# All transfers of a grouped-attention backward kernel on GpSimd's queue, small scalings on VectorE

## The chip, the cores and the metric

The kernel runs on one core of one Trainium2 chip. The metric is the device time of one execution in microseconds. The kernel before was run six times: 726.22 to 735.26, median 733.89. One further execution was profiled; every line of a profile below is from it.

A core has five instruction streams: TensorE (PE: matrix products and transposes; its weight loads are shown as PEld), VectorE (DVE), ScalarE (ACT), GpSimd (POOL) and SyncE (SP). Each runs its own instructions in order and waits on semaphores for the others. Transfers between main memory (HBM) and the on-chip memory SBUF are issued by an engine into a queue and carried out by 16 DMA engines that all queues share. In this kernel SP's transfers go out on a queue that the profile lists as "hardware_dynamic" (q1) and GpSimd's on one that it lists as "software_dynamic" (q0).

## The reference

Attention with 32 query heads that share 4 key/value heads, and its gradients:

```
B, Hq, Hkv, Sq, Sk, D = 32, 32, 4, 4, 2048, 128
scores = einsum("bhqd,bhkd->bhqk", q, repeat(k)) * D ** -0.5
p      = softmax(scores)
out    = einsum("bhqk,bhkd->bhqd", p, repeat(v))
out, vjp = jax.vjp(forward, q, k, v);  dq, dk, dv = vjp(grad_out)
```

It returns out, dq, dk and dv, all bf16. k, v, dk and dv are 32 x 4 x 2048 x 128, 67 MB each: 136 MB are read and 136 MB written. q, grad_out, out and dq are small.

## The kernel before

**The work.** One batch is one pass. Its 32 x 4 query rows fill the 128 partitions, 32 rows for each key/value head. A batch loads q and grad_out (`LQ`, two transfers of 32 KB, lines 430 and 432), four k tiles and four v tiles (`LK`, `LV`, 512 KB each, line 438: 128 rows of 4096 bytes). TensorE transposes k and v (`KT`, `VT`, line 452), multiplies scores (`S`, line 463), VectorE takes the maximum (`MX`, line 470), ScalarE the exponential (`EX`, line 479), VectorE the sum of each row and its reciprocal rinv (`L`, lines 483 and 485). Then come out (`O`, line 514), delta, the row sum of out times grad_out (`DL`, line 529), dp (`DP`, line 463), ds (`DS`, line 536), and dq, dv and dk.

The division by the softmax's sum is folded into small operands. `dop` is grad_out times rinv (line 488), `qp` is q times rinv times the scale (line 491), `rs` is rinv times the scale (line 495), a single column. `dop` is an operand of every dv product, `qp` of every dk product (`DV`, `DK`, line 551), and `rs` scales dq when it leaves PSUM (`DQe`, lines 521 and 523). All three are computed on GpSimd.

The products land in PSUM (eight banks). VectorE and ScalarE share the copies from there to SBUF: `KTe`, `VTe`, `ETe`, `DTe` (lines 420 and 423) and the casts of dv and dk (`DVe`, `DKe`, line 556: 128 x 1024, f32 to bf16). A batch's dv and dk leave in two stores of 1 MB each (`DVs`, `DKs`, line 560: 128 partitions, two rows of 4096 bytes each), its out and dq in one of 32 KB each (`Os`, `DQs`, line 525).

**The order.** `plan` runs once, when the program is built: it simulates the units of all 32 batches against due times (`DUE`), buffer counts (`CAP`) and costs (`OCC`), and returns one list of units. `emit` writes each unit's instructions in the order of that list, so the list sets the order on every engine. Work of neighbouring batches overlaps: the dk products of one batch run beside the scores of the next.

Transfers of one queue stand in the order of the list. SP has q, grad_out, k, v, dv and dk, 14 a batch; in the steady state one batch's worth is q, go, one v, two dv, four k, three v, two dk. GpSimd has per batch qp, dop, rs, the store of out and the store of dq. Of the transfers of one queue each waits, besides what its own buffers need, for the completion of the eighth transfer before it. SP waits in order: while it stands at a store whose casts are not done, the loads behind it are not issued.

Of the kernel before, what the change touches and what calls it, by code (L numbers as in the profile page):

```python
# [13 lines left out]
ALU = mybir.AluOpType  # L14
# [350 lines left out]
def kernel(  # L365
# [11 lines left out]
    nc = tc.nc  # L377
# [7 lines left out]
    scale = float(D) ** -0.5  # L385
# [18 lines left out]
    q_r, go_r, o_r, dq_r = rows(q), rows(grad_out), rows(out_0), rows(out_1)  # L404
    k_r, v_r, dk_r, dv_r = keys(k), keys(v), pairs(out_2), pairs(out_3)
    flat = lambda t: t[:].rearrange("p c d -> p (c d)")
# [18 lines left out]
    def emit(u):  # L425
        b, name, arg = u.key[0], u.key[1], u.key[2:]
        t = T[b]
        if name == "LQ":
            t["q"] = sm_pool.tile([P, D], BF16, name="q_sb")
            nc.sync.dma_start(out=t["q"][:], in_=q_r[b])  # L430
            t["go"] = sm_pool.tile([P, D], BF16, name="go_sb")
            nc.sync.dma_start(out=t["go"][:], in_=go_r[b])
        elif name in ("LK", "LV"):
            h, = arg
            p_, src = (k_pool, k_r) if name == "LK" else (v_pool, v_r)
            x = p_.tile([P, C, D], BF16, name="k_sb" if name == "LK" else "v_sb")
            t[name[1], h] = x
            nc.sync.dma_start(out=flat(x), in_=src[b, h])
        elif name == "QT":
            ps = t["qtp"] = bank(b, "qt", dt=BF16)  # L440
            nc.tensor.transpose(out=ps[:, 0, :], in_=t["q"][:], identity=ident[:])
# [11 lines left out]
        elif name in ("KTe", "VTe"):  # L453
            copy16(u.on, t[(name[:2],) + arg][:], t[(name[:2] + "p",) + arg][:])
        elif name in ("S", "DP"):
            c, = arg
            i, w = c // 2, c % 2
            if w == 0:
                t[name, i] = bank(b, name, i, n=2)
            x, side = ("KT", 0) if name == "S" else ("VT", 1)  # L460
            for h in range(NH):
                r = slice(32 * h, 32 * h + 32)
                nc.tensor.matmul(t[name, i][r, QW * w:QW * w + QW], lhsT=t["qdt"][:, side, r],  # L463
                                 rhs=t[x, h, i][:, CPQ * w:CPQ * w + CPQ, :],
                                 start=True, stop=True, tile_position=(0, 32 * h))
        elif name == "MX":
            i, = arg
            m = sm_pool.tile([P, 1], FP32, name="m", tag=f"m{i}")
            junk = junk_pool.tile([P, 2 * QW], BF16, name="mjunk")
            nc.vector.tensor_scalar(out=junk[:], in0=t["S", i][:], scalar1=-scale,  # L470
                                    scalar2=t["m"][:] if i else None, op0=ALU.mult, op1=ALU.min,
                                    accum_out=m[:])
            t["m"] = m
        elif name == "EX":
            i, = arg
            if i == 0:
                t["e"] = e_pool.tile([P, Sk], BF16, name="e_sb")
                t["l2"] = sm_pool.tile([P, 2], FP32, name="l2")
            nc.scalar.activation(out=t["e"][:, 2 * QW * i:2 * QW * i + 2 * QW], in_=t["S", i][:], func=ACT.Exp,  # L479
                                 bias=t["m"][:], scale=scale, accum_out=t["l2"][:, i:i + 1])  # L480
        elif name == "L":
            l = sm_pool.tile([P, 1], FP32, name="l")
            nc.vector.reduce_sum(out=l[:], in_=t["l2"][:], axis=AX.X)  # L483
            t["rinv"] = sm_pool.tile([P, 1], FP32, name="rinv")
            nc.vector.reciprocal(out=t["rinv"][:], in_=l[:])
        elif name == "dop":
            t["dop"] = sm_pool.tile([P, D], BF16, name="dop_sb")
            nc.gpsimd.tensor_scalar(out=t["dop"][:], in0=t["go"][:], scalar1=t["rinv"][:], scalar2=None, op0=ALU.mult)
        elif name == "qp":
            t["qp"] = sm_pool.tile([P, D], BF16, name="qp_sb")  # L490
            nc.gpsimd.tensor_scalar(out=t["qp"][:], in0=t["q"][:], scalar1=t["rinv"][:], scalar2=scale,
                                    op0=ALU.mult, op1=ALU.mult)
        elif name == "rs":
            t["rs"] = sm_pool.tile([P, 1], FP32, name="rs")
            nc.gpsimd.tensor_scalar(out=t["rs"][:], in0=t["rinv"][:], scalar1=scale, scalar2=None, op0=ALU.mult)
        elif name in ("ET", "DT"):
            i, = arg
            src = t["e"] if name == "ET" else t["ds"]
            t[name, i] = (et_pool if name == "ET" else dst_pool).tile([P, 8, P], BF16, name=name.lower() + "_sb")
            ps = t[name + "p", i] = bank(b, name, i, dt=BF16)  # L500
            for j in range(8):
                c = 8 * i + j
                nc.tensor.transpose(out=ps[:, j, :], in_=src[:, P * c:P * c + P], identity=ident[:])  # L503
        elif name in ("ETe", "DTe"):
            copy16(u.on, t[(name[:2],) + arg][:], t[(name[:2] + "p",) + arg][:])
        elif name in ("O", "DQ"):
            i, = arg
            if i == 0:
                t[name] = bank(b, name)
            xt, x = ("ET", "V") if name == "O" else ("DT", "K")  # L510
            for c in range(4 * i, 4 * i + 4):
                for h in range(NH):
                    r = slice(32 * h, 32 * h + 32)
                    nc.tensor.matmul(t[name][r, 0:D], lhsT=t[xt, c // 8][:, c % 8, r], rhs=t[x, h][:, c, :],  # L514
                                     start=(c == 0), stop=(c == C - 1), tile_position=(0, 32 * h))
        elif name in ("Oe", "DQe"):
            x, by = ("o", "rinv") if name == "Oe" else ("dq", "rs")
            t[x] = sm_pool.tile([P, D], BF16, name=x + "_sb")
            src = t[name[:-1]][:, 0:D]
            if u.on == "ACT":  # L520
                nc.scalar.activation(out=t[x][:], in_=src, func=ACT.Copy, scale=t[by][:])
            else:
                nc.vector.tensor_scalar(out=t[x][:], in0=src, scalar1=t[by][:], scalar2=None, op0=ALU.mult)  # L523
        elif name in ("Os", "DQs"):
            nc.gpsimd.dma_start(out=(o_r if name == "Os" else dq_r)[b], in_=t["o" if name == "Os" else "dq"][:])  # L525
        elif name == "DL":
            junk = junk_pool.tile([P, D], BF16, name="junk")
            t["dl"] = sm_pool.tile([P, 1], FP32, name="delta")
            nc.vector.tensor_tensor_reduce(out=junk[:], in0=t["o"][:], in1=t["go"][:], scale=1.0, scalar=0.0,
                                           op0=ALU.mult, op1=ALU.add, accum_out=t["dl"][:])  # L530
        elif name == "DS":
            i, = arg
            if i == 0:
                t["ds"] = ds_pool.tile([P, Sk], BF16, name="ds_sb")
            w = slice(2 * QW * i, 2 * QW * i + 2 * QW)
            nc.vector.scalar_tensor_tensor(out=t["ds"][:, w], in0=t["DP", i][:], scalar=t["dl"][:],  # L536
                                           in1=t["e"][:, w], op0=ALU.subtract, op1=ALU.mult)
        elif name in ("DV", "DK"):
            i, = arg
            if i == 0:  # L540
                for g in range(2):
                    t[name, "out", g] = o_pool.tile([P, 2, C, D], BF16, name=name.lower() + "_sb", tag="out")
            accs = [bank(b, name, i, g, n=2) for g in range(2)]
            t[name, i] = accs
            lhs, rhs = ("e", "dop") if name == "DV" else ("ds", "qp")
            for j in range(CPQ):
                c = CPQ * i + j
                for h in range(NH):
                    r = slice(32 * h, 32 * h + 32)
                    w = QW * (h % 2) + P * j  # L550
                    nc.tensor.matmul(accs[h // 2][:, w:w + P], lhsT=t[lhs][r, P * c:P * c + P],  # L551
                                     rhs=t[rhs][r, :], start=True, stop=True, tile_position=(32 * h, 0))
        elif name in ("DVe", "DKe"):
            i, g = arg
            copy = nc.scalar.copy if u.on == "ACT" else nc.vector.tensor_copy
            copy(out=t[name[:2], "out", g][:, :, CPQ * i:CPQ * i + CPQ, :].rearrange("p h c d -> p h (c d)"),  # L556
                 in_=t[name[:2], i][g][:].rearrange("p (h w) -> p h w", h=2))
        elif name in ("DVs", "DKs"):
            g, = arg
            nc.sync.dma_start(out=(dv_r if name == "DVs" else dk_r)[b, g],  # L560
                                in_=t[name[:2], "out", g][:].rearrange("p h c d -> p h (c d)"))

    with tc.manual_schedule():
# [29 lines left out]
```

## Time and profile before

| What | us |
|---|---|
| median of six runs | 733.89 |
| the profiled execution, whole | 732.28 |
| its span | 730.1 |
| VectorE busy | 578.0 |
| ScalarE busy | 589.6 |
| TensorE busy, matrix products | 608.2 |
| GpSimd busy | 75.9 |

The span runs from the first to the last instruction of the program; the whole time has 2.2 us more around it. Busy times can lie beside one another. Columns in a group of instructions are line, engine, operation, output and inputs with shapes, count, then busy time and mean of one, then the time that the engine idled just before them and what ended it. "issue" stands for time in which an engine waited for nothing that the profile shows. The TensorE clock was granted at 0.973 of full speed over the span.

The instructions that the change moves, from the groups of GpSimd:

```profile
L525 POOL DMA_DIRECT2D out_dram<-o_sb x32 | 19.6, 611 | 80.5 <-ACT o_sb L521 80.5
L488 POOL TENSOR_SCALAR dop_sb<-go_sb,rinv 128x128 bf16<-128x128 bf16 x32 | 19.5, 609 | 2.9
L525 POOL DMA_DIRECT2D out_dram<-dq_sb x32 | 17.3, 540 | 306.9 <-DVE dq_sb L523 191.9 <-ACT dq_sb L521 115.0
L495 POOL TENSOR_SCALAR rs<-rinv 128x1 f32<-128x1 f32 x32 | 7.1, 223 | 2.7
```

and the transfers, with their count, size and median time from issue to landing:

```profile
k_sb<-in_k_dram SPq DMA_DIRECT2D x128, 512.0 KB, 8.6
v_sb<-in_v_dram SPq DMA_DIRECT2D x128, 512.0 KB, 10.1
out_dram<-dv_sb SPq DMA_DIRECT2D x64, 1024.0 KB, 7.9
out_dram<-dk_sb SPq DMA_DIRECT2D x64, 1024.0 KB, 10.1
out_dram<-o_sb POOLq DMA_DIRECT2D x32, 32.0 KB, 5.9
out_dram<-dq_sb POOLq DMA_DIRECT2D x32, 32.0 KB, 6.7
```

### The profile page before, as it was taken

How to read it: one execution, taken by the hardware profiler on the slowest of the kernel's cores; microseconds unless marked ns; L12 is line 12 of the kernel's file. 1: busy time of each engine (PE TensorE's matmuls, PEld its weight loads, DVE VectorE, ACT ScalarE, POOL GpSimd, SP SyncE). 2: the span in 40 equal slices, each digit the busy share in tenths (PEclk: the TensorE clock that was granted, in tenths of full speed). 3: DMA queues.
4: the chain of work that ended last, by engine and by line, in shares of the span. 5: the costliest groups of instructions: out<-in, count | busy, mean ns of one | idle time of the engine just before them, and what ended most of it. 6: DMA issues, size and time to landing. Idle time of an engine off the chain costs nothing.

```text
span 730.1 us, 32386 instructions
## 1 busy us (share of the span) xinstructions
PE 608.2 (83%) x14400; PEld 453.9 (62%) x14400; DVE 578.0 (79%) x750; ACT 589.6 (81%) x947; POOL 75.9 (10%) x166
## 2 busy tenths in 40 slices
PE   6888888877889889888887988878888798988884
PEld 5666666665667666665665666666666665666662
DVE  2878887778878889887788887878887787988892
ACT  4788898788878889887888888788887887978883
POOL 0110110010100101110111100111100010101010
PEclk9999999999999999999999999999999999999995
DMA  9999999999999999999999999999999999999965
GB/s 338 336 380 384 388 391 402 358 401 380 366 389 343 407 408 395 408 398 394 394 402 394 362 411 385 390 394 392 372 376 343 396 403 361 358 403 406 390 243 211
DMA packets 83084, 274.73 MB, mean 376 GB/s; under 512 B 16384, under 2 KB 16384, under 8 KB 82944
## 3 DMA queue, kind: packets, MB, share of 16 engines
q1 hardware_dynamic: 80896, 270.56, 96.2%
q8 instruction: 112, 1.84, 1.0%
q0 software_dynamic: 2048, 2.10, 0.8%
q14 instruction: 28, 0.23, 0.1%
HBM read 136.31 MB, written 136.31 MB: 373 GB/s over the span
## 4 chain that ended last, share of the span: by engine, by line
PE 56%; ACT 19%; issue 14%; DMA 5%; DVE 3%; POOL 0%; POOLq 0%; SPq 0%; ACTq 0%; DVEq 0%
PE psum L452 29%; PE psum L463 9%; PE psum L551 9%; PE psum L514 7%; ACT dk_sb L556 6%; ACT e_sb L479 5%; ACT dv_sb L556 4%; DMA k_sb<-in_k_dram 3%; PE psum L503 2%; ACT vt_sb L420 1%; DMA out_dram<-dv_sb 1%; ACT kt_sb L420 1%; DVE ds_sb L536 1%; ACT dt_sb L420 1%; DMA v_sb<-in_v_dram 1%
## 5 line engine op out<-in xcount | busy, mean ns | idle before, releaser
L556 DVE CAST dk_sb<-psum 128x1024 bf16<-128x1024 f32 x128 | 153.7, 1222 | 43.1 <-PE psum L551 40.7
L556 DVE CAST dv_sb<-psum 128x1024 bf16<-128x1024 f32 x128 | 155.9, 1220 | 26.4 <-PE psum L551 23.3
L452 PE MATMUL psum<-ident,k_sb 128*128 128x128 bf16 x2048 | 153.6, 223 | 17.4 <-issue 9.2
L420 ACT COPY kt_sb<-psum 128x512 f32<-128x512 f32 x231 | 131.9, 601 | 35.3 <-PE psum L452 31.9
L452 PE MATMUL psum<-ident,v_sb 128*128 128x128 bf16 x2048 | 146.8, 222 | 10.8 <-issue 10.7
L452 PEld LDWEIGHTS <-k_sb 128*128 128x128 bf16 x2048 | 120.3, 100 | 49.9 <-issue 31.3
L556 ACT CAST dk_sb<-psum 128x1024 bf16<-128x1024 f32 x128 | 127.0, 1024 | 27.2 <-PE psum L551 26.8
L452 PEld LDWEIGHTS <-v_sb 128*128 128x128 bf16 x2048 | 122.3, 99 | 39.6 <-issue 33.3
L556 ACT CAST dv_sb<-psum 128x1024 bf16<-128x1024 f32 x128 | 132.4, 1035 | 11.9 <-PE psum L551 11.3
L420 ACT COPY vt_sb<-psum 128x512 f32<-128x512 f32 x194 | 108.3, 590 | 30.4 <-PE psum L452 29.9
L536 DVE SCALAR_TENSOR_TENSOR ds_sb<-psum,delta,e_sb 128x1024 bf16<-128x1024 f32 x64 | 82.0, 1282 | 20.1 <-PE psum L463 18.0
L551 PE MATMUL psum<-qp_sb,ds_sb 32*128 32x128 bf16 x2048 | 62.0, 220 | 22.0 <-DVE l L483 8.4
L551 PE MATMUL psum<-dop_sb,e_sb 32*128 32x128 bf16 x2048 | 60.9, 219 | 14.5 <-issue 9.5
L479 ACT ACTIVATE e_sb<-psum,m 128x1024 bf16<-128x1024 f32 x64 | 72.1, 1127 | 0.4 <-DVE mjunk L470 0.4
L551 PEld LDWEIGHTS <-ds_sb 32*128 32x128 bf16 x2048 | 37.0, 94 | 43.7 <-issue 30.4
L514 PE MATMUL psum<-k_sb,dt_sb 128*32 128x128 bf16 x2048 | 48.1, 226 | 12.4 <-issue 11.8
L551 PEld LDWEIGHTS <-e_sb 32*128 32x128 bf16 x2048 | 34.6, 93 | 36.7 <-issue 23.0
L503 PE MATMUL psum<-ident,ds_sb 128*128 128x128 bf16 x512 | 40.6, 223 | 12.3 <-DVE ds_sb L536 9.9
L525 POOL DMA_DIRECT2D out_dram<-dq_sb x32 | 17.3, 540 | 306.9 <-DVE dq_sb L523 191.9
L503 PE MATMUL psum<-ident,e_sb 128*128 128x128 bf16 x512 | 39.9, 221 | 9.7 <-ACT dk_sb L556 8.2
L470 DVE TENSOR_SCALAR_CACHE_REDUCE mjunk<-psum,m 128x1024 bf16<-128x1024 f32 x32 | 41.1, 1284 | 7.9 <-PE psum L463 6.8
L423 DVE COPY vt_sb<-psum 128x1024 bf16<-128x1024 bf16 x62 | 42.3, 682 | 4.5 <-PE psum L452 4.5
(72 smaller groups left out, 558.7 us busy)
## 6 DMA issues: line engine op xcount, KB each, us to landing
k_sb<-in_k_dram SPq DMA_DIRECT2D x128, 512.0 KB, 8.6
v_sb<-in_v_dram SPq DMA_DIRECT2D x128, 512.0 KB, 10.1
out_dram<-dv_sb SPq DMA_DIRECT2D x64, 1024.0 KB, 7.9
out_dram<-dk_sb SPq DMA_DIRECT2D x64, 1024.0 KB, 10.1
q_sb<-in_q_dram SPq DMA_DIRECT2D x32, 32.0 KB, 10.3
go_sb<-in_grad_out_dram SPq DMA_DIRECT2D x32, 32.0 KB, 9.1
out_dram<-o_sb POOLq DMA_DIRECT2D x32, 32.0 KB, 5.9
out_dram<-dq_sb POOLq DMA_DIRECT2D x32, 32.0 KB, 6.7
```

The lines of the kernel that those rows point to most:

```text
L420: nc.scalar.copy(out=out.rearrange("p c d -> p (c d)").bitcast(FP32), in_=in_.rearrange("p c d -> p (c d)").bitcast(FP32))
L423: nc.vector.tensor_copy(out=out, in_=in_)
L452: nc.tensor.transpose(out=ps[:, j, :], in_=t[x, h][:, 8 * i + j, :], identity=ident[:])
L463: nc.tensor.matmul(t[name, i][r, QW * w:QW * w + QW], lhsT=t["qdt"][:, side, r], rhs=t[x, h, i][:, CPQ * w:CPQ * w + CPQ, :], start=True, ...
L470: nc.vector.tensor_scalar(out=junk[:], in0=t["S", i][:], scalar1=-scale, scalar2=t["m"][:] if i else None, op0=ALU.mult, op1=ALU.min, accu ...
L479: nc.scalar.activation(out=t["e"][:, 2 * QW * i:2 * QW * i + 2 * QW], in_=t["S", i][:], func=ACT.Exp, bias=t["m"][:], scale=scale, accum_o ...
L503: nc.tensor.transpose(out=ps[:, j, :], in_=src[:, P * c:P * c + P], identity=ident[:])
L514: nc.tensor.matmul(t[name][r, 0:D], lhsT=t[xt, c // 8][:, c % 8, r], rhs=t[x, h][:, c, :], start=(c == 0), stop=(c == C - 1), tile_positio ...
L525: nc.gpsimd.dma_start(out=(o_r if name == "Os" else dq_r)[b], in_=t["o" if name == "Os" else "dq"][:])
L536: nc.vector.scalar_tensor_tensor(out=t["ds"][:, w], in0=t["DP", i][:], scalar=t["dl"][:], in1=t["e"][:, w], op0=ALU.subtract, op1=ALU.mult)
L551: nc.tensor.matmul(accs[h // 2][:, w:w + P], lhsT=t[lhs][r, P * c:P * c + P], rhs=t[rhs][r, :], start=True, stop=True, tile_position=(32 * ...
L556: copy(out=t[name[:2], "out", g][:, :, CPQ * i:CPQ * i + CPQ, :].rearrange("p h c d -> p h (c d)"), in_=t[name[:2], i][g][:].rearrange("p ...
```

## The change

All transfers that SP issued are issued by GpSimd, on the queue that already carried the stores of out and dq; SP issues none. The three small scalings go from GpSimd to VectorE. The plan, its costs and the order of the list are the same, so every unit stands where it stood in the list: GpSimd's queue gets the 16 transfers of a batch in the order of the list (out, q, go, one v, two dv, four k, three v, dq, two dk), and VectorE's queue gets 96 more instructions. In nearly every batch these stand as qp, dop, rs between the first and the second cast of dk that follow the reciprocal. The queues of TensorE and ScalarE are the same instructions in the same order.

```
         if name == "LQ":
-            nc.sync.dma_start(out=t["q"][:], in_=q_r[b])
+            nc.gpsimd.dma_start(out=t["q"][:], in_=q_r[b])
...
-            nc.sync.dma_start(out=t["go"][:], in_=go_r[b])
+            nc.gpsimd.dma_start(out=t["go"][:], in_=go_r[b])
         elif name in ("LK", "LV"):
...
-            nc.sync.dma_start(out=flat(x), in_=src[b, h])
+            nc.gpsimd.dma_start(out=flat(x), in_=src[b, h])
...
         elif name == "dop":
-            nc.gpsimd.tensor_scalar(out=t["dop"][:], in0=t["go"][:], scalar1=t["rinv"][:], scalar2=None, op0=ALU.mult)
+            nc.vector.tensor_scalar(out=t["dop"][:], in0=t["go"][:], scalar1=t["rinv"][:], scalar2=None, op0=ALU.mult)
         elif name == "qp":
-            nc.gpsimd.tensor_scalar(out=t["qp"][:], in0=t["q"][:], scalar1=t["rinv"][:], scalar2=scale,
+            nc.vector.tensor_scalar(out=t["qp"][:], in0=t["q"][:], scalar1=t["rinv"][:], scalar2=scale,
                                     op0=ALU.mult, op1=ALU.mult)
         elif name == "rs":
-            nc.gpsimd.tensor_scalar(out=t["rs"][:], in0=t["rinv"][:], scalar1=scale, scalar2=None, op0=ALU.mult)
+            nc.vector.tensor_scalar(out=t["rs"][:], in0=t["rinv"][:], scalar1=scale, scalar2=None, op0=ALU.mult)
...
         elif name in ("DVs", "DKs"):
-            nc.sync.dma_start(out=(dv_r if name == "DVs" else dk_r)[b, g],
+            nc.gpsimd.dma_start(out=(dv_r if name == "DVs" else dk_r)[b, g],
                                 in_=t[name[:2], "out", g][:].rearrange("p h c d -> p h (c d)"))
```

## The prediction

> **What bounds the kernel now.** I read the engine table and the DMA table first, then the waits of TensorE, then the chain, then the timeline around the instructions that move.
>
> ```profile
> span 730.1 us, 32386 instructions
> PE 608.2 (83%) x14400; PEld 453.9 (62%) x14400; DVE 578.0 (79%) x750; ACT 589.6 (81%) x947; POOL 75.9 (10%) x166
> q1 hardware_dynamic: 80896, 270.56, 96.2%
> q0 software_dynamic: 2048, 2.10, 0.8%
> PE 56%; ACT 19%; issue 14%; DMA 5%; DVE 3%; POOL 0%; POOLq 0%; SPq 0%; ACTq 0%; DVEq 0%
> ```
>
> Two things look full. The SP ring (q1) fills 96.2% of the sixteen DMA engines, and the chain that ended last is 56% TensorE, 19% ScalarE, 14% issue. They are told apart by who waits for whom. In the waits of TensorE between 30 and 700 us no load appears; over the whole span this is the only one that matters:
>
> ```profile
> PE psum L514 <- issue: 20.6, 20, 2.2
> PE psum L452 <- issue: 20.0, 21, 1.8
> PE psum L452 <- DMA k_sb<-in_k_dram: 6.8, 3, 5.7
> ```
>
> Columns: us in total, times, longest. 5.7 of the 6.8 us is the very first load. Setting the packet records of q1 against the issue order, I find that K loads end a median 7.2 us and V loads 11.2 us before their first transpose, 19 in 20 of them at least 4.9 us before. VectorE and ScalarE wait for no output buffer either. So the compute engines set the period of about 22 us per batch, and the DMA engines keep pace with little to spare: between 30 and 700 us they idle 12.9 us, 1.9%.
>
> Now the place where instructions move, in batch 16:
>
> ```profile
> 368.04 0.16 DVE L485 RECIPROCAL rinv<-l 128x1 f32<-128x1 f32 x1
> 368.44 2.36 DVE L556 CAST dk_sb<-psum 128x1024 bf16<-128x1024 f32 x2 [0.24 <-PE psum L551]
> 368.92 0.61 POOL L488 TENSOR_SCALAR dop_sb<-go_sb,rinv 128x128 bf16<-128x128 bf16 x1
> 369.61 0.22 POOL L495 TENSOR_SCALAR rs<-rinv 128x1 f32<-128x1 f32 x1
> 369.72 0.40 PE L551 MATMUL psum<-dop_sb,e_sb 32*128 32x128 bf16 x16
> 369.73 1.49 SPq L560 DMA_DIRECT2D out_dram<-dk_sb  x2
> ```
>
> Columns: start, length. GpSimd has dop ready at 369.53, while VectorE is in the first dk cast (1.22 us, to about 369.65). TensorE starts DV 0.07 us after that cast, which frees its PSUM bank. GpSimd is just early enough; nothing waits for it.
>
> **Scalings to VectorE.** GpSimd loses 32 each of 0.37, 0.61 and 0.22 us, 38 us that nobody waited for. VectorE's queue in the changed program has qp, dop and rs between the first and the second dk cast, in nearly every batch. Their length on VectorE is not in the trace. From below, the reciprocal on one column from SBUF takes 0.164 us; from above, the dq scaling of 128x128 out of PSUM 0.351 us. I take 0.20 for qp and dop, near the lower row since operands lie in SBUF and the reciprocal has the same fixed part, and 0.164 for rs. Consecutive VectorE instructions overlap by about 0.08 us (the dt copy starts at 366.65, runs 0.69, the next starts at 367.26), so a batch gains 0.12 + 0.12 + 0.08 = 0.32 us; bounds 0.25 and 0.63. DV starts 0.24 us later, and the second dk cast and all behind it 0.32 us. VectorE is 79% busy, but here, from 365.85 to 373.27, its only gap is the 0.24 us ahead of the first dk cast, and TensorE is busy 1.83 us of the two from 370 to 372, so this delay has no cover on the spot. How much reaches the end depends on the chain. In batch 15 the chain goes ScalarE, TensorE L503 (346.77), then this DV matmul at 347.82: passed in full. In batch 16 it goes through ScalarE's copies (369.52 to 370.24): partly absorbed. I take three quarters: 32 x 0.32 x 0.75 = 7.7 us; from 4 (low bound, half) to 20 us (high bound, all).
>
> **Transfers to GpSimd's queue.** 448 of the 512 leave SP; GpSimd issues all 512, 16 a batch. Its price is in the rows for o and dq: 607 and 540 ns for 128 rows, never longer than 749, though VectorE was 79% busy. The stores of 256 rows I put at twice that, 1.1 us; a batch then takes 12 x 0.58 + 4 x 1.1 = 11.4 us of 22: covered by GpSimd's idle time. Per transfer it is slower than SP where SP was not held (0.39 to 0.43 us), and an idle ring's first packet comes 1.33 us after the issue (the first o store) against 0.9 us for SP's stores. Loads have their 4.9 us of margin for this. The stores' landing frees buffers nobody waits for. The first dv store of a batch finds the ring nearly empty in a third of the batches (0.9 us from issue to packet), so there the DMA engines idle 0.4 to 1.1 us longer; that uses up DMA margin, not compute time. I cost it at nothing; without that margin it would be some 10 x 0.75 = 8 us.
>
> In the one queue o stands ahead of q, go and v, and dq ahead of dk. A late o would hold them: o's issue at 371.97 is 0.66 us after q's at 371.31, within the margin; dq at 382.77 follows the v loads as before. Every transfer also waits for the completion of the eighth before it, as on SP now. With small ones among them the smallest window (dq, dk, dk, o, q, go, v, dv) holds 3.8 MB, 9.3 us at the 408 GB/s of full slices, longer than the 5.9 us and 6.7 us that small stores now need to land: the ring does not run dry from this. The q and go loads change from 18 ns packets of 256 bytes to the software ring's packets of 2048 bytes at 84 ns, 9.3 to 5.4 us per engine. That widens the DMA margin to 16.8 us and takes nothing off compute.
>
> **Ends.** GpSimd's first load comes after the identity's memset (0.92 against 0.73 us) and 0.3 us slower to its packet: +0.5 us. The last dk stores need 1.1 us instead of 0.39 to issue: +1 us.
>
> Sum: 7.7 + 0.5 + 1.0 = 9.2 us on the profiled execution's own 732.28 (730.1 span and 2.2 around it): 741.5. The median of the six runs is 1.6 above that execution, so 743.
>
> A rule against the change stands in the Trainium skill, "SBUF — State Buffer", section "SBUF: two separate sides": a VectorE instruction in a two-port mode and GpSimd's descriptor writing lock each other out of a shared port, whichever starts first. The steady 540 and 607 ns agree that today's VectorE work, which reads PSUM, does not do this; by the rule the new scalings, SBUF to SBUF, could, and either side could wait. The sum by it would be rival B below; mine is without it.
>
> **Rivals.**
>
> *A, the sum above, 0.46*: 737 to 752, slower by 1.3% at its middle.
>
> *B, the software ring costs more, 0.23.* Either GpSimd writes the dk store's descriptors (released at 369.73) just as dop comes up on VectorE, and dop waits the 1.1 us: 32 x 1.1 = 35 us, 743 + 35 = 778. Or packets are slower. A 4096-byte packet takes 159 ns on q1, the small stores' 2048 bytes 84 ns on q0 with 19 in 20 at that value, so nothing in the trace speaks for it; but q1's 4096-byte packets fill 689 us per engine, so 5% more is 34 us, less the margin of 16.8: 751 at most on top of no other delay, and 10% gives 786. The Trainium skill, "DMA: Bandwidth & Descriptors", section "Latency and other measured facts", says that engines 7 and 15 are usually slower with the software ring, as a guess at the cause; the uniform 84 ns here does not show it.
>
> *C, faster, 0.22: TensorE waits less for its instructions.* "issue" is 14% of the chain, 102 us, and the instruction queue moved 112 packets of 16 KB, one for each such wait: about 0.9 us each. They share the engines with the data. A small store on another ring than q1 sees its first packet a median 4.35 us after issue, 1.33 when q1 is empty: q1 keeps some 3 us ahead of others. If the software ring keeps less ahead, a third off these waits is 34 us: 743 - 34 = 709. It decides from about 0.1 us per fetch on, which pays for A. Against it: what queues may lie in the engine, not in the ring, and then nothing changes; it could also keep more ahead.
>
> *D, no change, 0.09*: the delay of DV is taken up in later gaps (TensorE idles 0.8 of 2 us from 360 to 362): 732 to 740.
>
> **How the numbers follow.** About 1% is what a measurement here can tell from no change (the six runs lie between 726 and 735), so slower begins at 741.2. Of A 0.32 lies above and 0.14 below; B is all above; C all but 0.01 below 726.6; D gives 0.07 of same and 0.02 of faster. Slower 0.55, same 0.22, faster 0.23. The likeliest is A, 743. The range leaves a tenth on each side, half of C and half of B: 720 to 772.
>
> **What would show it.** Right: VectorE near 596 us busy with 96 more instructions of 0.16 to 0.2 us; dop ending after the first dk cast and DV starting after dop; TensorE's issue share unchanged; POOL's issues near 0.55 and 1.1 us; 4096-byte packets at 159 ns on q0; loads still ahead of their use. Wrong: dop or qp over 0.5 us (B), packets over 165 ns and TensorE waiting for k_sb (B), issue under 12% of the chain (C), or TensorE waiting for loads because GpSimd stands at a store.

## The result and the profile after

The changed kernel takes 739.31 us (median of 10 runs, 735.16 to 747.27); the kernel before, run beside it, 733.89 us (20 runs, 725.39 to 738.74). The ratio is 1.0097, interval 1.0058 to 1.0136. Ratios here and below are of means over the fast runs, of which that of 747.27 is not one, so they can differ a little from the ratio of the medians. A second set on another chip, among the experiments below, gave 1.0134 (1.0084 to 1.0184). So it is slower by about one per cent, 5 to 9 us; 743 had been predicted. That is just under the bound of 741.2 which the prediction had drawn between no change (to which it gave 0.22) and slower (0.55).

The profiled execution took 733.87 us, 5.4 less than its median. It is good for the lengths of single instructions and poor for a difference of 1%. First the engine table and the queues of its page:

```profile
span 732.1 us, 32273 instructions
PE 602.6 (82%) x14400; PEld 448.8 (61%) x14400; DVE 588.4 (80%) x846; ACT 592.5 (81%) x947; POOL 297.4 (41%) x518
q0 software_dynamic: 75776, 272.66, 96.7%
q8 instruction: 112, 1.84, 1.0%
q14 instruction: 28, 0.23, 0.1%
```

All data is on q0, which fills the DMA engines as q1 did. VectorE has 10.4 us more work and GpSimd 221 more, nearly all of it issuing. The chain of waits can't be set against the one of before: in this profile the followed chain covers only 2% of the span. TensorE's waits between 30 and 700 us can (line and releaser: us in total, times, longest):

```profile
PE psum L452 <- issue: 20.2, 19, 2.1
PE psum L514 <- issue: 19.8, 20, 2.1
PE psum L551 <- issue: 16.6, 18, 1.8
...
PE psum L551 <- DVE dop_sb L488: 5.9, 15, 0.6
...
PE psum L551 <- DVE rs L495: 2.4, 7, 0.3
```

The waits for dop and rs are new; both stand ahead of DV products. There is still no wait for a load. The lines of L452 and L514 are as before (20.0 and 20.6), and so is that of L551, which in the kernel before read:

```profile
PE psum L551 <- issue: 16.4, 17, 1.9
```

So the change took nothing off the waits put down to "issue". The moved scalings, from the groups by line (count, then busy us and mean ns), and the longest issues of GpSimd:

```profile
L488 DVE TENSOR_SCALAR dop_sb<-go_sb,rinv 128x128 bf16<-128x128 bf16 x32 | 8.0, 249 | 0.0
L491 DVE TENSOR_SCALAR qp_sb<-q_sb,rinv 128x128 bf16<-128x128 bf16 x32 | 7.9, 246 | 0.0
L495 DVE TENSOR_SCALAR rs<-rinv 128x1 f32<-128x1 f32 x32 | 4.7, 147 | 0.0
```

```profile
L438 POOL DMA_DIRECT2D k_sb<-in_k_dram x128 | 68.2, 538 | 49.6 <-PE psum L514 38.8
L560 POOL DMA_DIRECT2D out_dram<-dv_sb x64 | 45.7, 719 | 114.2 <-DVE dv_sb L556 86.4
L560 POOL DMA_DIRECT2D out_dram<-dk_sb x64 | 45.7, 714 | 112.9 <-ACT et_sb L420 38.8
```

And the place in batch 16, from the timeline (start, length):

```profile
368.45 0.16 DVE L485 RECIPROCAL rinv<-l 128x1 f32<-128x1 f32 x1
368.85 1.22 DVE L556 CAST dk_sb<-psum 128x1024 bf16<-128x1024 f32 x1 [0.24 <-PE psum L551]
369.99 0.24 DVE L491 TENSOR_SCALAR qp_sb<-q_sb,rinv 128x128 bf16<-128x128 bf16 x1
370.15 0.25 DVE L488 TENSOR_SCALAR dop_sb<-go_sb,rinv 128x128 bf16<-128x128 bf16 x1
370.31 0.15 DVE L495 TENSOR_SCALAR rs<-rinv 128x1 f32<-128x1 f32 x1
370.37 1.21 DVE L556 CAST dk_sb<-psum 128x1024 bf16<-128x1024 f32 x1
370.45 0.40 PE L551 MATMUL psum<-dop_sb,e_sb 32*128 32x128 bf16 x16 [0.33 <-DVE dop_sb L488]
```

dop ends at 370.40 and TensorE's product starts at 370.45: a wait of 0.33 us that the kernel before did not have. Over batches 2 to 30 the first DV product starts a median 1.84 us after the reciprocal's end, 1.49 before.

### The profile page after: what moved, and what is told of

Same layout as the page of the kernel before. It is cut to its first block, busy times and chain, and to the rows that moved or that the text cites. A ratio compares the mean times of both kernels' runs of the same rounds, so it can differ in the third digit from the quotient of the medians.

```text
span 732.1 us, 32273 instructions
## 1 busy us (share of the span) xinstructions
PE 602.6 (82%) x14400; PEld 448.8 (61%) x14400; DVE 588.4 (80%) x846; ACT 592.5 (81%) x947; POOL 297.4 (41%) x518
## 3 DMA queue, kind: packets, MB, share of 16 engines
q8 instruction: 112, 1.84, 1.0%
## 5 line engine op out<-in xcount | busy, mean ns | idle before, releaser
L556 DVE CAST dk_sb<-psum 128x1024 bf16<-128x1024 f32 x128 | 156.3, 1222 | 49.2 <-PE psum L551 44.5
L452 PE MATMUL psum<-ident,k_sb 128*128 128x128 bf16 x2048 | 153.9, 224 | 22.2 <-issue 12.5
L452 PEld LDWEIGHTS <-k_sb 128*128 128x128 bf16 x2048 | 121.0, 100 | 57.3 <-issue 37.2
L452 PE MATMUL psum<-ident,v_sb 128*128 128x128 bf16 x2048 | 144.8, 221 | 7.9 <-issue 7.7
L452 PEld LDWEIGHTS <-v_sb 128*128 128x128 bf16 x2048 | 120.8, 99 | 37.5 <-issue 23.5
L556 ACT CAST dv_sb<-psum 128x1024 bf16<-128x1024 f32 x128 | 130.8, 1023 | 10.0 <-PE psum L551 6.6
L560 POOL DMA_DIRECT2D out_dram<-dv_sb x64 | 45.7, 719 | 114.2 <-DVE dv_sb L556 86.4
L560 POOL DMA_DIRECT2D out_dram<-dk_sb x64 | 45.7, 714 | 112.9 <-ACT et_sb L420 38.8
L438 POOL DMA_DIRECT2D k_sb<-in_k_dram x128 | 68.2, 538 | 49.6 <-PE psum L514 38.8
L438 POOL DMA_DIRECT2D v_sb<-in_v_dram x128 | 67.5, 530 | 47.8 <-DMA out_dram<-dv_sb 22.8
L551 PE MATMUL psum<-qp_sb,ds_sb 32*128 32x128 bf16 x2048 | 61.8, 218 | 24.5 <-DVE l L483 10.1
L551 PE MATMUL psum<-dop_sb,e_sb 32*128 32x128 bf16 x2048 | 58.8, 217 | 20.2 <-issue 7.8
L551 PEld LDWEIGHTS <-ds_sb 32*128 32x128 bf16 x2048 | 36.7, 93 | 44.8 <-issue 31.2
L514 PE MATMUL psum<-k_sb,dt_sb 128*32 128x128 bf16 x2048 | 48.0, 224 | 16.5 <-issue 15.5
L551 PEld LDWEIGHTS <-e_sb 32*128 32x128 bf16 x2048 | 34.2, 92 | 39.4 <-issue 16.6
```

The source lines that it names most:

```text
L438: nc.gpsimd.dma_start(out=flat(x), in_=src[b, h])
L452: nc.tensor.transpose(out=ps[:, j, :], in_=t[x, h][:, 8 * i + j, :], identity=ident[:])
L560: nc.gpsimd.dma_start(out=(dv_r if name == "DVs" else dk_r)[b, g], in_=t[name[:2], "out", g][:].rearrange("p h c d -> p h (c d)"))
```

## The experiments

Twelve kernels in three sets, each set on a chip of its own with the kernel before beside it (730.93, 730.45 and 729.88 us). Theory: the scalings between the dk casts cost most, the queue little. Rivals: the queue costs, at the two ends or in every batch.

**The scalings alone.** The loads and stores stay on SP; only lines 488, 491 and 495 change from `nc.gpsimd` to `nc.vector`.

> The kernel before with only the three scalings moved to VectorE; SP keeps its queue. Theory (the cost is VectorE's, the queue is free): 5 to 9 us over the kernel before, ratio 1.007 to 1.012, like the full change (1.0097); dop ends about 0.3 us after the first dk cast and DV starts after it. Rival (the queue costs, VectorE's additions vanish in its gaps): within 2 us of the kernel before, ratio 0.997 to 1.003. A ratio between 1.003 and 1.007 says that both have a share.

734.31 us, 1.003 (0.9999 to 1.006). The theory misses: DV starts at 1.84 after the reciprocal here too, in full, and it costs 0 to 4 us. The middle lies at the upper edge of the rival's range.

**The queue alone.** The changed kernel with the three scalings back on GpSimd.

> The changed kernel with the three scalings back on GpSimd, where they now stand in one queue with all transfers, between the dq store and the dk stores. Theory (the queue costs 3 to 5 us at the two ends, VectorE's additions 2): ratio 1.003 to 1.009, unless the dq store, which in the changed kernel waits for an earlier store's completion until 368.4, keeps dop back: then dop ends 0.5 us or more after the first dk cast, with no more than 5 us on top. Rival (the software ring itself slows the steady state): as much as the changed kernel, 1.008 or more, with a period of a batch over 22.3 us in the profile.

740.8 us, 1.0144 (1.0105 to 1.0182). dop is in time (1.18 us after the reciprocal, DV at 1.49), TensorE has no wait for dop, and the kernel is as slow as with both edits. The period of a batch is 22.43 us in its profile, 22.13 before. The rival holds, and together the two runs turn the split of the sum around.

**dop as early as it can be.** In the changed kernel's list, dop goes right behind the reciprocal and qp and rs ahead of the ds of the batch; q gets a pool of six buffers.

```
...
+     for u in order:
...
+         if u.key[1:] == ("DS", 0):
+             moved += [by_key[b, "qp"], by_key[b, "rs"]]
+         moved.append(u)
+         if name == "L":
+             moved.append(by_key[b, "dop"])
...
```

> The changed kernel with dop placed directly behind the reciprocal, into the 0.24 us in which VectorE waits for the dk products, and qp and rs directly ahead of ds (q_sb gets six buffers in place of four, since qp now reads it later). Theory: the delay of DV goes, 0.3 us a batch; what is left is 0.25 us of qp and rs that meet VectorE's wait for dp: 4 to 8 us under the changed kernel, ratio to the kernel before 0.999 to 1.004. Rival (the queue costs): no change from 1.0097, 1.006 or more.

738.28 us, 1.0102 (1.0068 to 1.0137). dop now ends 0.29 us after the reciprocal's end and the wait for it is gone; the time is not. The lateness of dop is not what costs.

**More scalings.** dop is computed three times, the two first into spare tiles.

```
+             for spare in range(2):
+                 x2 = sm_pool.tile([P, D], BF16, name=f"spare{spare}")
+                 nc.vector.tensor_scalar(out=x2[:], in0=t["go"][:], scalar1=t["rinv"][:], scalar2=None, op0=ALU.mult)
```

> The changed kernel with dop computed three times, two of them into spare tiles ahead of the real one: 64 more VectorE instructions of 0.25 us, overlapping by 0.08, so DV starts 0.34 us later still in each of 32 batches, 10.9 us. Theory (three quarters of it reach the end): 6 to 11 us over the changed kernel, ratio to the kernel before 1.018 to 1.025. Rival (VectorE's delays are absorbed): within 3 us of the changed kernel, 1.006 to 1.014.

Each spare scaling puts dop off by some 0.17 us, the step from qp to dop in the timeline above: 10.9 us in all. 740.56 us, 1.0136 (1.01 to 1.0172), against 1.0097 and 1.0134 for the changed kernel: some 3 us of the 10.9 arrive, or none. The trace shows who pays. TensorE's waits between 30 and 700 us:

```profile
PE psum L452 <- issue: 16.4, 18, 2.1
PE psum L517 <- issue: 15.6, 15, 2.2
PE psum L554 <- DVE dop_sb L491: 15.4, 23, 0.9
PE psum L554 <- issue: 13.3, 13, 2.0
```

(L517 and L554 are L514 and L551, moved by the three lines.) The wait for dop grew from 5.9 to 15.4 us, and the waits put down to "issue" fell by nearly as much. All its waits for issue and for dop together are 63.9 us before, 66.3 with the early dop, 64.7 with the scalings alone, 65.5 after and 66.1 here. With those put down to rs, which end at the same product, they are 63.9, 66.3, 67.3, 67.9 and 70.7: most of the delay is paid out of the issue waits, not all of it. The account of TensorE's time further down shows that these are waits for its next block of instructions; a later dop uses the same time.

**Many more scalings.** dop nine times, the same edit with `range(8)`.

> The changed kernel with dop computed nine times, eight of them into spare tiles ahead of the real one: DV starts 8 x 0.17 = 1.36 us later in each batch, 43 us in all. Theory (a delay of TensorE is paid out of its wait for the next 256 instructions, which is 0.5 to 1.3 us long, and what goes beyond is passed on): more than half now reaches the end, 22 to 40 us over the changed kernel, ratio 1.04 to 1.065, with the waits that follow an instruction packet well under 95 us. Rival (a quarter is passed on whatever its size, as two spare ones showed): 8 to 14 us, 1.02 to 1.03.

763.1 us, 1.0434 (1.0368 to 1.0501): 24 us above the changed kernel for 43.5 us by which dop is put off (8 x 0.17 x 32). The time is the theory's, but the way to it is another one:

```profile
PE psum L554 <- DVE dop_sb L491: 36.7, 22, 1.9
PE psum L554 <- DVE rs L498: 11.4, 7, 1.6
...
PE psum L452 <- issue: 8.5, 9, 1.9
PE psum L554 <- issue: 8.0, 8, 1.7
```

```profile
span 758.7 us, 32529 instructions
PE 622.6 (82%) x14400; PEld 468.1 (62%) x14400; DVE 630.3 (83%) x1102; ACT 593.3 (78%) x947; POOL 298.2 (39%) x518
```

```profile
core 0: 758.7 us, clock 0.937
```

The waits for dop and rs grew by 40 us, and the waits for instructions shrank by nearly as much. All idle time of TensorE together is only 3 to 6 us above that of the changed kernel's two profiles; what grew by 19 to 20 us is its busy time, at a granted clock of 0.937 (0.934 to 0.948 in the four runs) where the changed kernel had 0.963 to 0.982. The clock stood at half speed for some 96 us of this profile and for 26 and 29 us of those two. So nearly the whole delay was still covered, and most of the 24 us came as longer busy time at the lower clock. That the late dop brought the clock down is likely, since nothing else in the kernel differs, but no run shows how.

**Fewer bytes.** The changed kernel stores only the first of the two rows that each dv and dk store carries: half of dv and half of dk are left out, the casts are all made.

```
-            nc.gpsimd.dma_start(out=(dv_r if name == "DVs" else dk_r)[b, g],
-                                in_=t[name[:2], "out", g][:].rearrange("p h c d -> p h (c d)"))
+            nc.gpsimd.dma_start(out=(dv_r if name == "DVs" else dk_r)[b, g][:, 0],
+                                in_=t[name[:2], "out", g][:, 0].rearrange("p c d -> p (c d)"))
```

> The changed kernel with each dv and dk store sending only the first of its two rows: half of dv and dk is left out, 67 of 273 MB. Theory (the compute engines set the period and the DMA engines keep pace): within 1% of the changed kernel, 732 to 744 us, with the DMA engines idle a quarter of the time. Rival (the DMA engines set the period): 15 us or more less, below 724, down to what the compute engines need.

689.6 us, 0.9425 (0.9385 to 0.9465). The theory's view of the bound falls with this: the compute engines had the same work and the kernel became 6% faster. Its page and its TensorE waits (30 to 700 us):

```profile
span 688.8 us, 32273 instructions
PE 593.5 (86%) x14400; PEld 445.9 (65%) x14400; DVE 586.7 (85%) x846; ACT 591.0 (86%) x947; POOL 272.0 (39%) x518
...
q0 software_dynamic: 59392, 205.55, 80.7%
```

```profile
PE psum L452 <- issue: 10.5, 10, 1.7
...
PE psum L551 <- issue: 5.4, 6, 1.8
PE psum L514 <- issue: 3.2, 6, 1.0
```

The three issue lines fall from 56.6 to 19.1 us. That these are waits for instructions can be seen from where they fall. The instruction queue q8 moved 112 packets of 16 KB; for TensorE's 28800 weight loads and products that is 256 instructions of 64 bytes in each. With these numbered in the order of their start, most of TensorE's pauses of over half a microsecond (55 of 65 before) stand at one and the same place in every 256. It idled 65.2 us there before, 60.3 in the changed kernel and 21.2 here, and 55, 45 and 17 of the 112 crossings cost it more than half a microsecond. Where the DMA engines have room, TensorE gets its instructions in time more often. Of the 43 us between the spans of the two profiles, 39 are these pauses and 9 are busy time, at a granted clock of 0.989 against 0.982; other idle time grew by 5. The edit also shortens 128 issues of GpSimd by 0.18 us each; no wait of TensorE was put down to them before.

**Fewer bytes and more scalings.** The same with dop three times.

> The run with half of dv and dk left out, with dop computed three times on VectorE (two more scalings a batch, some 0.5 us of delay for the first dP product in each, 15 us of VectorE in all). Theory (a delay on VectorE is paid out of TensorE's waits for its next block of instructions, and with a quarter less DMA traffic these waits are half as long): the cover is thinner, so more passes on than the 1.3 us that the same addition cost in the changed kernel: 4 to 10 us over the run without it, ratio 0.947 to 0.956. Rival (the cover is other slack, the same in both): 0 to 2.5 us, ratio 0.942 to 0.946.

692.75 us, 0.9504 (0.9472 to 0.9536); the two intervals do not touch. Here the 10.9 us cost 0.8%, some 6 us, where the full kernel let through some 3 or none. The cover for a late dop is thinner when TensorE waits less for instructions, as the theory had it. (The product that is delayed is the first DV product, not the dP product that the expectation names.)

**TensorE's time in these profiles.** Busy with loads or products, idle where a block of 256 instructions ends, and idle elsewhere, in us:

| Kernel | span | busy | idle at a block's end | other idle | granted clock |
|---|---|---|---|---|---|
| before | 730.1 | 610.3 | 65.2 | 54.6 | 0.973 |
| scalings alone | 730.7 | 608.3 | 60.8 | 61.6 | 0.975 |
| the changed kernel | 732.1 | 604.6 | 60.3 | 67.2 | 0.982 |
| the changed kernel, again | 736.8 | 606.0 | 63.8 | 67.0 | 0.980 |
| dop early | 738.7 | 611.4 | 67.2 | 60.1 | 0.972 |
| dop three times | 739.0 | 610.3 | 52.1 | 76.6 | 0.972 |
| dop nine times | 758.7 | 624.9 | 23.3 | 110.5 | 0.937 |
| fewer bytes | 688.8 | 595.8 | 21.2 | 71.8 | 0.989 |
| fewer bytes, dop three times | 694.8 | 595.7 | 16.6 | 82.5 | 0.990 |

A later dop turns idle time at a block's end into other idle time. With all bytes moved the sum of the two changes little (127.5 and 130.8 us in the changed kernel, 128.7 with two spare scalings, 133.8 with eight); with fewer bytes it grows by 6 us for two.

**Stores alone and loads alone.** From the kernel before, once only the dv and dk stores (line 560), once only the loads (430, 432, 438) go to GpSimd's queue.

> The kernel before with the dv and dk stores alone moved to GpSimd's queue: loads on SP, all stores on GpSimd, scalings on GpSimd among them. Loads no longer stand behind a store that waits for its casts, and the engines take loads and stores in turn. Theory (the period hangs on TensorE's waits for instructions, which depend on how full the DMA engines are, not on who issues): within 1.5% of the kernel before, 0.985 to 1.01. Rival (the single order is the limit): 2% or more faster, with the DMA engines' idle time in the middle under 5 us.

> The kernel before with its loads alone on GpSimd's queue; the dv/dk stores stay on SyncE's, the scalings on GpSimd. Theory (the ends): only the head is late, by 2 to 3.5 us, the tail is as before: ratio 1.003 to 1.006. Rival (a cost in every batch of the loads' lateness on GpSimd's ring): 1.009 to 1.017. If it is the stores alone that cost, as the run with the stores alone on GpSimd's queue (1.0127) would have it, this is within 1.003 and the head's loss is made up later.

Stores alone: 739.52 us, 1.0127 (1.0086 to 1.0168). Loads alone: 737.89 us, 1.0119 (1.0075 to 1.0163). Both theories miss, and of the loads' rivals the cost in every batch is what was measured. Each half costs as much as the whole, within these intervals. The explanations by a sum fail with this, those by the ends too: with the loads alone only the head is late (first S product at 15.9 us against 12.8), with the stores alone only the tail (batch 31's S to the end 37.0 us against 35.3).

**The ends back on SP.** First only the k and v loads of batch 0, the q and grad_out loads of batches 0 to 2 and the last batch's four stores; then all loads of batches 0 to 2 and those stores (the second is shown; its q and grad_out loads are edited like the k and v loads).

```
-            nc.gpsimd.dma_start(out=flat(x), in_=src[b, h])
+            (nc.sync if b < 3 else nc.gpsimd).dma_start(out=flat(x), in_=src[b, h])
...
-            nc.gpsimd.dma_start(out=(dv_r if name == "DVs" else dk_r)[b, g],
+            (nc.sync if b == B - 1 else nc.gpsimd).dma_start(out=(dv_r if name == "DVs" else dk_r)[b, g],
```

> The changed kernel with the first loads (k and v of batch 0, q and grad_out of batches 0 to 2) and the last batch's four stores back on SP; 493 of 512 transfers stay on GpSimd. Theory (the queue costs at the ends alone): the first scores product starts at 12.8 to 13.5 us, not at 15.3, the part behind the last batch's first scores is 35 to 36 us and not 36.3 to 37.4, and the ratio falls from 1.0097 to 1.002 to 1.007. Rival (the queue costs in the steady state): ratio 1.008 or more, though the first scores start early.

> The changed kernel with every load of batches 0 to 2 and the last batch's four dv/dk stores on SyncE's queue again, all else on GpSimd's. Theory (what the queue costs lies at the two ends): the first S product is back at 12.8 to 13.2 us, the part from batch 31's S to the end back at 35 to 35.6 us, and of the 7 us some 3.5 to 5 go: ratio 1.002 to 1.006. Rival (the queue costs something in every batch, 0.1 to 0.25 us of each): the two ends are as before and the ratio stays 1.008 to 1.014, with the excess in the periods of batches 2 to 30.

The first was a bad experiment: 747.44 us, 1.0238 (1.0197 to 1.0279), because batch 1's loads on GpSimd's queue ran beside those of batch 0 on SP's and the last k tile of batch 0 landed at 15.4 us instead of 9.4; the first S product came at 21.1 us. The second did what it should at the ends: first S product at 13.6 us (15.3 and 14.2 in the two profiles of the changed kernel), end part 35.1 us (36.3 in both). The time is 738.9 us, 1.0113 (1.0069 to 1.0157): no gain that shows, as the rival had it. What the ends gave back was lost in the middle.

**The changed kernel once more.**

> The changed kernel once more, beside the others on the same chip: 1.007 to 1.013. Every theory expects this; it shows by how much a ratio of one program moves between two sets of runs, and so which of the differences between 1.010 and 1.0144 seen so far mean anything. If it comes out at 1.013 or above, the difference between the changed kernel and the one with the scalings back on GpSimd (1.0144) means nothing.

738.68 us, 1.0134 (1.0084 to 1.0184). The same program moves between 1.0097 and 1.0134 from set to set, and its period over batches 2 to 30 is 22.09 us in one profile and 22.31 in the other. So the differences among the queue's variants, 1.010 to 1.0144, mean nothing, and no single profile resolves 0.2 us per batch.

No version that moves all the bytes and has transfers moved to GpSimd's queue came out faster than the kernel before.

**An account of the DMA engines.** The page's table of queues gives the time that packets took as a share of the engines' span. Summed over the queues and taken off the span (profiled executions, us):

| Kernel | span | packets | span less packets |
|---|---|---|---|
| before | 730.1 | 716.2 | 13.9 |
| scalings alone | 730.7 | 715.4 | 15.3 |
| the changed kernel | 732.1 | 716.0 | 16.1 |
| the changed kernel, again | 736.8 | 715.4 | 21.4 |
| loads alone | 739.2 | 716.3 | 22.9 |
| stores alone | 735.9 | 719.7 | 16.2 |
| queue alone | 743.1 | 717.1 | 26.0 |
| ends back on SP | 737.2 | 715.1 | 22.1 |
| fewer bytes | 688.8 | 564.1 | 124.7 |

A DMA engine has on average 715 to 720 us of packets in every kernel of this table that moves all the bytes, and the kernel before took 730. The last column is less than the idle time, because packets overlap: up to 23 of them were in flight on the 16 engines before, 17 us of overlap in all, so the engines idled some 31 us, 18 of it in the first and the last 30. The slower kernels have either more time without packets or, with the stores alone, more packet time. This is an account and not yet a cause: a late compute engine also leaves the DMA engines idle.

One rival can be set aside with the lists of waits. Each transfer waits for the eighth before it, and one queue now holds all of them: in the changed kernel GpSimd stood some 78 us at transfers whose wait ended with an earlier one's completion, SP before some 14. With the loads alone or the stores alone it is at most 7 us on either queue, and the cost is as large.

## Why the prediction was right, and where it was not

The sum was right to 4 us and its sign held; the range contained the time. Its terms were not.

*The bound.* "The compute engines set the period", with the DMA engines' 12.9 us of idle time and the loads' 4.9 us taken as margin: this step failed. The observations hold (no wait for a load, before or after), but with a quarter of the data traffic gone the kernel takes 6% less. A full set of DMA engines shows here in TensorE's waits for instructions (60 us at the ends of blocks, 21 with fewer bytes), the "issue" lines that the prediction quoted and counted to compute.

*Scalings on VectorE, 7.7 us.* Durations were undersized (0.246 to 0.249 us for qp and dop against 0.20 taken, 0.147 for rs), the delay of DV was 0.35 us rather than 0.24, and dop came after the first dk cast as predicted. "Three quarters passed" is what failed: the scalings alone cost 0 to 4 us, and computing dop in time gained nothing. "This delay has no cover on the spot" overlooked the wait for the next instruction block, which takes up most of it. The mechanism of rival D, a delay taken up in later gaps, was the true one here.

*Transfers, "I cost it at nothing".* This is the term that was wrong. The queue alone costs 1.0144, 8 to 13 us, where 1.5 us (1.002) had been put down for it with both ends. The prediction had named one mechanism and priced it at 8 us "without that margin": a dv store that refills dry engines. It is there. Where the engines had run dry, the first packet of the dv store came some 0.9 us after the start of its issue on SP (0.91 in the kernel before, 0.89 with the loads alone) and 1.27 to 1.30 on GpSimd. Such a place in the second profile of the changed kernel, in stretches of time (columns: the stretch, its length, then busy us and instructions of PE, PEld, DVE, ACT and POOL, then the granted clock, the DMA engines' busy share and GB/s):

```profile
470.00:472.00 2.00, 2.00 (x22) 2.00 (x20) 1.38 (x2) 0.97 (x2) 0.00 (x0) 0.50 1.04 400
472.00:473.80 1.80, 1.80 (x53) 1.49 (x52) 0.85 (x2) 1.70 (x3) 0.00 (x0) 1.00 0.65 254
473.80:475.80 2.00, 2.00 (x80) 1.58 (x77) 1.86 (x3) 1.61 (x3) 1.33 (x2) 1.00 0.11 39
```

Two microseconds of nearly empty DMA engines, ended by the two dv stores, the only instructions of GpSimd there. Such places go along with the cost: between 30 us and 32 us before the end, stretches of over 0.4 us with at most four packets in flight add up to 2.7 us in the kernel before, 1.4 with the scalings alone and 1.2 in the first profile of the changed kernel, whose period (22.09 us) is no longer than before (22.13). In its second profile (22.31) they are 4.8 us, with the loads or the stores alone 4.5 and 5.2, with the queue alone 8.0 and with the ends back on SP 9.9 (periods 22.28 to 22.43). But there are only three to six of them in a run, and 0.4 us of later refill at each is 1 to 2.4 us. The loads alone cost as much while their dv stores stayed on SP. So what the queue costs in the steady state is measured (5 to 11 us, from the run with the ends back on SP) and its cause is not settled: why the engines run dry more, and why either half of the transfers costs the whole, stays open.

*Lengths at the queue.* 0.55 us per 128-row transfer was right (0.53 to 0.56); for 256 rows it was 0.72, not 1.1. Packets kept 159 ns in the median. GpSimd's issues fit, as said.

*Ends, +0.5 and +1.* The tail was +1.0 as predicted, though a store's issue took 0.71 us there and not the 1.1 that the sum had. The head was +1.4 to +2.5 us: GpSimd's first load is issued at 1.30 us, not 0.92, because the identity's memset is followed by a second instruction (line 199 of masks.py, 1.00 to 1.29 us in the profile before). But giving both back gained nothing, so they are no terms to be added to the rest.

*Rival B*, dop waiting for descriptor writing or slower packets: not seen. qp, dop and rs each kept one length within 10 ns over the run, and the issue of 256 rows stayed between 699 and 732 ns. The rule of the Trainium skill, "SBUF — State Buffer", section "SBUF: two separate sides", by which either could be locked out, has no trace in these numbers; only 5 of the 96 scalings met an issue in time, by 21 ns at most, so they do not refute it. *Rival C*, shorter waits for instructions by a change of ring: the waits did not move (56.6 us in three lines after, 57.0 before), though their size and nature were as it said. Its price of 709 us was hardly within reach: the packets alone take 716 us, some 712 without the 3.9 us that the larger q and grad_out packets were to save. It is no strict floor, since packets overlap by 17 us.

So the prediction came out right because two errors cancelled: 7.7 us for the scalings against 0 to 4, and 1.5 us for queue and ends against 8 to 13. That the time was hit is luck.

## What to carry to other kernels

Add up the packets' shares of the DMA engines before asking which engine waits: with 98% taken, loads that land early prove no margin, because the instruction blocks wait in the same engines and the loss appears as "issue" of TensorE. A delay of a third of a microsecond ahead of TensorE cost 0 to 4 us in 32 batches, because TensorE waited for its instructions anyway; test that by doubling the delay before paying for it in a sum, and set busy time and granted clock of the two profiles side by side before calling the rest passed on. Do each half of a change alone, and distrust one profile for a difference under 1%.

## What was not expected of the hardware

Crossing from one block of 256 instructions to the next cost TensorE more than half a microsecond of idle time at 45 to 55 of its 112 blocks, 60 to 67 us of some 730 in all, in the kernels with all bytes and no spare scalings. The Trainium skill, "Runtime: NRT & Kernel Launch", section "Instruction fetch mechanics", describes these 16 KB blocks and says that the cost of crossing is mostly hidden. The runs disagree where the DMA engines are full, and agree better with room in them (17 blocks and 21 us with 82% taken).

Software and hardware rings moved packets at one rate: 159 ns in the median for 4096 bytes on either, 168 to 169 ns in the mean with all large transfers on one queue.

The scatter from run to run goes with the granted TensorE clock, which lay between 0.963 and 0.986 in the runs with all bytes and up to two spare scalings: a fit of one line per program over them gives 4.0 us of span for 0.01 of clock (give or take 1.0). At equal clock the scalings alone cost 2.9 us (give or take 1.4), the queue alone 8.6 (1.9) and both together 8.2 (1.3): not a sum of the two. The loads alone cost 6.0 (1.9) and the stores alone 6.5 (2.4). Outside that range lay the runs with fewer bytes (0.985 to 0.992) and those with dop nine times (0.934 to 0.948).
